# A new written order for the attention stage of a fused attention and mixer kernel

## The chip, the cores and the metric

The kernel runs on one core of a Trainium2 chip. What counts is the device time of one execution in microseconds (us), here the median of three runs. The core has five engines with their own queues, each in order: TensorE (matmuls), VectorE, ScalarE, GpSimd and SyncE (which only starts transfers).

## The reference

Three blocks follow each other, for 2 batches, 768 positions and 512 features.

```python
# 1. attention, 8 heads of 64: keys and queries count only within one hash bucket
mask = q_bucket[:, :, :, None] == k_bucket[:, :, None, :]      # 6 sign bits of x @ proj
scores = np.where(mask, scale * q @ k.T, -1e9)
attn = exp(scores - max) / (sum + 1e-9);  x = attn @ v
# 2. first mixer
xk, xr = mu * x + (1 - mu) * x_prev                            # x_prev: one position earlier
x = sigmoid(xr @ w_r) * (relu(xk @ w_k) ** 2 @ w_v)
# 3. second mixer: x @ w_in, norm, product over positions with w_spatial, gate, @ w_out
```

## The kernel before

Everything is fp32; a product of weights is made of three fp32r products of high and low parts (`mm3`). The weights come as float64 words and are unpacked on the chip by eight steps (`weight_jobs`): load, magnitude (ScalarE), clamp, shift, top (VectorE), first (ScalarE), power, low (VectorE), rest (two operations on GpSimd for the weights of attention's time, on VectorE later).

Attention goes over 8 pairs of heads, 12 units to a pair (2 halves of the queries x 2 heads x 3 blocks of 128 queries), 96 units in all. A group is six units. A unit is

- `scores` (S, line 394): 4 matmuls of 384 columns into one of two score banks `s`,
- `peak` (K, line 404, VectorE): scales the scores into `p` (three buffers) and takes the row's extreme; it frees the score bank,
- `expo` (X, line 416, ScalarE): the exponential in place, with its sum,
- `transp` (T, line 426): two groups of three 128x128 transposes, each group into one of three banks `t`; T2i and T2i+1 belong to unit i,
- `evac` (line 432): copies each bank `t` to `PT`, on ScalarE (E) or on VectorE (V).

When a group's units are evicted, `av3` (A, line 461) multiplies `PT` with the values: two calls per group, each 12 matmuls in the trace, into the one output bank `o`. `recip` (R) inverts the sums on VectorE and writes them to DRAM by four transfers, `spread` (D) reads them back to all partitions, and `finish` (F, line 473) multiplies the output bank into `XT` and frees it. For a coming pair there are loads of keys and queries to the `tk` tiles by GpSimd's queue (`load_pair`, four transfers), the raw load (`load_x`), the values (`load_v`), the hash bits (`bits_mm` Z, line 292, 8 matmuls into a bank `t`; `bits_signs` G on VectorE and GpSimd; `bits_place` B or P, transfers on SyncE's queue), and eight subtractions on GpSimd (`split_piece` Q, line 275).

The order of every queue is the order in which the program names the operations. Before, nine units are written out as a string `head`, and from the third period on a loop over periods of three units says

```python
scores(a); scores(a + 1); peak(a)
move(a - 2, 1); expo(a); move(a - 1, 0); move(a - 1, 1)
peak(a + 1); ...; expo(a + 1); av3(p - 3); ...
scores(a + 2); move(a, 0); move(a, 1); ...
```

where `move` is T and E in one; other jobs (weights, loads, mixing pieces of the first mixer) hang on slots of the periods (`plan`). After the loop the last products of attention stand among the first of the mixer (`r_products`). From then on jobs hang on ticks, one to each group of 12 matmuls of 512 columns.

Of the kernel before, what the change touches and what calls it, by code (L numbers as in the profile page):

```python
# [16 lines left out]
B, H, S, D = 2, 8, 768, 64  # L17
# [7 lines left out]
WARM_A, WARM_B = 6, 3  # L25
# [207 lines left out]
def attention(tc, nc, mid, wide, top, dram, ident, msc, omu, misc, cst_sb, pb, epsT, kq, vP, XT, TK0, wr, w_r, wk,  # L233
              w_k, w_v, ps_s, ps_t, obank, mix_jobs, r_products, r_sigmoid, tick, now, at_tick, plan_weight, wv, **_):
    PS = bass.MemoryType.PSUM
    with ExitStack() as ctx:
# [76 lines left out]
        def bits_signs(pp):  # L313
            bits_sign(pp)
            bits_scale(pp, nc.gpsimd)
# [103 lines left out]
            P[i] = c  # L419

        def transp(i, c):
            p = P[i] if c == 0 else P.pop(i)
            t = ps_t.tile([128, 512], F32, tag="t", name="t")
            for n in range(3):
                k0 = 128 * (3 * c + n)
                nc.tensor.transpose(t[:, 128 * n:128 * n + 128], p[:, k0:k0 + 128], ident)  # L426
            return t
# [48 lines left out]
                R.pop(g).rearrange("p n q -> p (n q)"),  # L476
            )

        plan = {}

        early = []

        def at_slot(p, k, job):
            plan.setdefault((p, k), []).append(job)

        def plan_early(p0, where):
            ld, jobs = weight_jobs(
                nc, mid, w_v[:128], lambda: (wv[0][:, 0, 0, :], wv[0][:, 1, 0, :]), nc.vector,
            )
            early.extend(jobs)  # L490
            plan_unit(p0, where, ld, jobs, (0, 1, 2, 3, 5, 6))
# [14 lines left out]

        np3 = nunits // 3
        units = [(wr, w_r, c, 0) for c in range(4)]
        units += [(wk, w_k, c, o) for o in (0, 512) for c in range(4)]
        late = ((-1, 1), (0, 0), (0, 0), (0, 0), (1, 0), (1, 0), (1, 0), (1, 0))  # L510
        soon = ((-1, 2), (-1, 0), (-1, 0), (0, 0), (1, 0), (1, 0), (1, 1), (1, 1))
        first = ((-1, 1), (0, 0), (0, 0), (1, 0), (1, 0), (1, 0), (3, 0), (1, 1))

        def plan_unit(p0, where, ld, jobs, keys=range(8)):
            at_slot(p0 - 3, 1, ld)
            for k in keys:
                at_slot(p0 + where[k][0], where[k][1], jobs[k])

        for n in range(12):
            dst, src, c, o = units[n]  # L520
            ld, jobs = weight_jobs(
                nc, mid, src[128 * c:128 * c + 128, o:o + 512],
                lambda dst=dst, c=c, o=o: (dst[:, 0, c, o:o + 512], dst[:, 1, c, o:o + 512]),
                nc.gpsimd,
            )
            plan_unit(4 + 2 * n, soon if n % 2 else late, ld, jobs)
        plan_early(np3 - 4, first)
        both, pieces = (nc.vector, nc.vector), []
        for c in range(4):
            for h, jobs in enumerate(mix_jobs(mid, 0, 0, c, 0, both + (nc.gpsimd,))):  # L530
                pieces.append(jobs)
        begun = (52, 53, 54, 57, 58, 59, 60, 61)
        ended = (55, 56, 57, 58, 59, 60, 61, 62)
        for k in range(2 * np3):
            for jobs, b, e in zip(pieces, begun, ended):
                if e == k:
                    at_slot(k // 2, k % 2, jobs[2])
            for jobs, b, e in zip(pieces, begun, ended):
                if b == k:
                    at_slot(k // 2, k % 2, jobs[0])  # L540
                    at_slot(k // 2, k % 2, jobs[1])
        gates1 = [jobs for c in range(4) for jobs in mix_jobs(mid, 1, 0, c, 4, both + (nc.vector,))]
        for pp in range(-1, npairs - 1):
            p0 = 4 * pp
            if pp >= 0:
                if pp:
                    at_slot(p0, 0, lambda n=pp + 1: load_pair(n))
                if pp:
                    at_slot(p0 + 1, 0, lambda n=pp + 1: bits_mm(n))
                    at_slot(p0 + 1, 0, lambda n=pp + 1: bits_signs(n))  # L550
                at_slot(p0 + 1, 1, lambda n=pp + 1: bits_place(n, (0, 1) if n > 1 else (0,)))
                at_slot(p0 + 3, 1, lambda n=pp + 1: load_v(n))
                for k in range(8):
                    at_slot(p0 + 1 + k // 4, k // 2 % 2, lambda n=pp + 1, k=k: split_piece(n, k))
            if 0 <= pp < npairs - 2:
                at_slot(p0 + 3, 0, lambda n=pp + 2: load_x(n))

        nc.scalar.dma_start(msc, misc)
        load_halves()
        clear(0, 0, nc.vector)  # L560
# [20 lines left out]
            for n in range(3):  # L581
                av(p // 2, 3 * (p % 2) + n)

        def move(i, c, copy=nc.scalar.copy):
            evac(i, c, transp(i, c), copy)

        ts = {}

        def group(k):
# [2 lines left out]
        def from_group(k, copy=nc.scalar.copy):  # L592
            evac(k // 2, k % 2, ts.pop(k), copy)

        def slot(n):
            for job in plan.pop((n // 10, n % 10), ()):
                job()

        step = {
            "S": scores, "K": peak, "X": expo, "T": group, "E": from_group,  # L600
            "V": lambda k: from_group(k, nc.vector.tensor_copy), "J": slot, "Z": bits_mm, "G": bits_signs,
            "L": lambda e: split_part(0, e, 0, nc.vector), "R": recip, "P": lambda e: bits_place(1, (e,)),
        }
        head = (
# [3 lines left out]
        )  # L608
        for w in head.split():
            step[w[0]](int(w[1:]))  # L610
            if w == "S1":
                warm(WARM_B)
        for p in range(3, np3):
            a = 3 * p
            scores(a)
            scores(a + 1)
            peak(a)
            if p > 3:
                move(a - 2, 1)
                expo(a)  # L620
                move(a - 1, 0)
                move(a - 1, 1)
            else:
                move(a - 1, 0)
                expo(a)
                move(a - 1, 1)
            peak(a + 1)
            for job in plan.pop((p, 2), ()):
                job()
            expo(a + 1)  # L630
            av3(p - 3)
            if p % 2 == 0:
                recip(p // 2 - 1)
            if p == 3:
                spread((p - 3) // 2, nc.gpsimd)
            for job in plan.pop((p, 0), ()):
                job()
            if p % 2 and p > 3:
                spread((p - 3) // 2, nc.sync)
            if p >= np3 - 2:  # L640
                tick()
            scores(a + 2)
            move(a, 0)
            move(a, 1)
            peak(a + 2)
            expo(a + 2)
            if p >= 4 and p % 2 == 0:
                finish((p - 4) // 2)
            move(a + 1, 0)
            for job in plan.pop((p, 1), ()):  # L650
                job()
            if p == np3 - 2:
                plan_wv()
            if p >= np3 - 2:
                tick()
        assert not any(p < np3 for p, _ in plan), plan

        def begin(*ns):
            for n in ns:
                gates1[n][0]()  # L660
                gates1[n][1]()

        def end(*ns):
            for n in ns:
                gates1[n][2]()

        o = r_products(0, 0)
        begin(0, 1)
        r_sigmoid(0, 0, o, top)
        move(nunits - 2, 1)  # L670
        move(nunits - 1, 0)
        move(nunits - 1, 1)
        recip(np3 // 2 - 1)
        begin(2)
        av3(np3 - 3)
        end(0, 1)
        begin(3)
        spread(np3 // 2 - 1, nc.sync)
        tick()
        o = r_products(0, 1)  # L680
        finish(np3 // 2 - 2)
        end(2, 3)
        begin(4, 5, 6)
        r_sigmoid(0, 1, o, top)
        tick()
        av3(np3 - 2)
        av3(np3 - 1)
        finish(np3 // 2 - 1)
        assert not plan, plan

    def rest_of_gates():
        end(4, 5, 6)
        begin(7)
        end(7)

    return rest_of_gates

# [311 lines left out]
```

## Time and profile before

| | us |
|---|---|
| median of 3 runs | 537.13 (537.05 to 537.41) |
| span of the profiled execution, first to last instruction | 534.7 |
| TensorE busy | 528.7 |
| VectorE busy | 366.8 |
| ScalarE busy | 333.9 |
| GpSimd busy | 142.0 |

Of the profiled execution the trace times the span alone; the median of the runs is 2.4 us longer. Attention takes the first 225 us of the span. A TensorE that is busy by the profile is not one at its peak, since matmuls are pipelined: the distance between the starts of two rows says what the first one costs.

### The profile page before, as it was taken

To read this page: it belongs to the slowest core of one execution; us is meant where nothing else is said; L and a number is where in the kernel's file an instruction comes from. 1 tells how busy PE (TensorE), PEld (TensorE's weight loads), DVE (VectorE), ACT (ScalarE), POOL (GpSimd) and SP (SyncE) were. 2 spreads that over 40 slices of the span, in tenths; PEclk is the share of its full clock that TensorE was granted. 3 is DMA by queue.
4 is the path that set the end of the run, shared out by engine and by line. 5 is a ranking of instruction groups with operands and counts; after the bars stand their busy time and mean duration, and the time that the engine had idled before them with its cause. 6 is when DMAs were issued, how large, how long until landed. Compare 5 with 4: busy or idle time off the path is not lost.

```text
span 534.7 us, 8278 instructions
## 1 busy us (share of the span) xinstructions
PE 528.7 (99%) x2886; PEld 425.4 (80%) x2886; DVE 366.8 (69%) x751; ACT 333.9 (62%) x702; POOL 142.0 (27%) x157
## 2 busy tenths in 40 slices
PE   8999999999999999999999999999999999999997
PEld 6777777777777677688888888888888889989896
DVE  8786969686868987699678587445784948734230
ACT  8988989898989799457666567364433543221221
POOL 7939494949494832000000000001100000000000
PEclk9999999999999999999999999999999999999999
DMA  8994929393939312110221021005343200010102
GB/s 224 151 236 97 254 74 242 88 254 80 242 92 247 87 40 56 55 39 2 78 71 55 34 78 48 32 1 167 109 163 106 76 0 1 0 40 21 59 21 99
DMA packets 20041, 51.06 MB, mean 95 GB/s; under 512 B 3776, under 2 KB 6656, under 8 KB 20000
## 3 DMA queue, kind: packets, MB, share of 16 engines
q1 hardware_dynamic: 13424, 31.17, 19.3%
q0 software_dynamic: 6144, 19.07, 17.5%
q8 instruction: 23, 0.38, 0.3%
q10 hardware_dynamic: 432, 0.28, 0.2%
q14 instruction: 18, 0.15, 0.1%
HBM read 46.29 MB, written 3.19 MB: 93 GB/s over the span
## 4 chain that ended last, share of the span: by engine, by line
PE 95%; DVE 2%; ACT 1%; issue 1%; DVEq 0%
PE o L183 14%; PE s L394 13%; PE v L764 12%; PE o L461 12%; PE t L426 11%; PE k L183 9%; PE s L183 7%; PE r L183 6%; PE w L183 6%; PE u L183 5%; PE z L292 1%; ACT p L416 1%; DVE p L404 1%; DVE tk L379 1%; DVE d L152 0%
## 5 line engine op out<-in xcount | busy, mean ns | idle before, releaser
L404 DVE TENSOR_SCALAR_CACHE_REDUCE p<-s 128x768 f32<-128x768 f32 x96 | 90.9, 955 | 37.0 <-PE s L394 34.4
L432 ACT COPY PT<-t 128x384 f32<-128x384 f32 x189 | 83.6, 479 | 20.2 <-PE t L426 20.0
L416 ACT ACTIVATE p<-p,m 128x768 f32<-128x768 f32 x96 | 90.7, 945 | 3.2 <-DVE p L404 2.3
L394 PE MATMUL s<-tk 128*128 128x384 f32 x384 | 85.0, 354 | 0.9 <-DVE p L404 0.4
L394 PEld LDWEIGHTS s<-tk 128*128 128x128 f32 x384 | 63.9, 188 | 19.7 <-issue 6.0
L426 PE MATMUL t<-ident,p 128*128 128x128 f32 x576 | 74.9, 273 | 0.5 <-ACT p L416 0.5
L426 PEld LDWEIGHTS t<-ident,p 128*128 128x128 f32 x576 | 66.6, 141 | 5.4 <-ACT p L416 1.7
L764 PE MATMUL v<-k,wv 128*128 128x512 f32 x288 | 68.9, 389 | 0.0
L461 PE MATMUL o<-PT,v 128*64 128x384 f32 x384 | 68.8, 494 | 0.0
L764 PEld LDWEIGHTS v<-k,wv 128*128 128x128 f32 x288 | 54.0, 188 | 11.2
L275 POOL TENSOR_TENSOR tk<-x,tk 64x384 fp32r<-64x384 f32 x56 | 58.9, 1079 | 1.0
L821 POOL DMA_DIRECT2D wsp<-in_w_spT_dram x6 | 3.3, 564 | 169.9 <-DVE w_a L45 155.3
L461 PEld LDWEIGHTS o<-PT,v 128*64 128x64 f32 x384 | 24.8, 136 | 28.6 <-issue 27.9
L750 DVE TENSOR_TENSOR k<-kt,k 128x512 fp32r<-128x512 f32 x24 | 16.6, 691 | 30.7 <-ACT k L749 30.6
L183 PE MATMUL k<-tk,wk 128*128 128x512 f32 x144 | 35.6, 389 | 0.0
L183 PE MATMUL o<-wk,tk 128*128 128x512 f32 (+1 forms) x162 | 34.9, 374 | 0.0
L130 ACT CAST tk<-g 128x384 fp32r<-128x384 f32 x16 | 8.2, 513 | 42.0 <-DVE g L896 42.0
L183 PEld LDWEIGHTS o<-wk,tk 128*128 128x128 f32 x162 | 28.9, 188 | 5.3
L183 PEld LDWEIGHTS k<-tk,wk 128*128 128x128 f32 x144 | 27.0, 188 | 5.6
L156 DVE SCALAR_TENSOR_TENSOR f<-XT,msc,d 128x256 f32<-128x256 f32 x48 | 24.5, 510 | 6.0 <-ACT d L150 4.6
L66 DVE SCALAR_TENSOR_TENSOR w_a<-w_raw,w_p 128x512 f32<-128x512 uint32 x32 | 26.6, 831 | 0.9
L183 PE MATMUL w<-wk,tk 128*128 128x512 f32 x114 | 26.5, 389 | 0.0
(131 smaller groups left out, 847.8 us busy)
## 6 DMA issues: line engine op xcount, KB each, us to landing
tk<-in_kq_dram POOLq DMA_DIRECT2D x30, 384.0 KB, 9.5
x<-in_kq_dram POOLq DMA_DIRECT2D x6, 768.0 KB, 5.6
w_raw<-in_w_k_dram SPq DMA_DIRECT2D x8, 512.0 KB
w_raw<-in_w_v_dram SPq DMA_DIRECT2D x8, 512.0 KB
w_raw<-in_w_in_dram SPq DMA_DIRECT2D x8, 512.0 KB
v<-in_vP_dram SPq DMA_DIRECT2D x8, 384.0 KB
rb<-ds SPq DMA_DIRECT2D x30, 96.0 KB
out_dram<-ot SPq DMA_DIRECT2D x11, 256.0 KB
```

What stands on the lines that cost most here:

```text
L66: nc.vector.scalar_tensor_tensor(st["a"].bitcast(F32), st["raw"][:, :, 0], 2.0 ** -52, st["p"].bitcast(F32), op0=ALU.mult, op1=ALU.mult,)
L156: nc.vector.scalar_tensor_tensor(st["f"], x, mu, st["d"], op0=ALU.mult, op1=ALU.add)
L183: nc.tensor.matmul(o, a, x, start=(i == 0), stop=(i == len(seq) - 1))
L275: nc.gpsimd.tensor_sub(tk[l, 1 + 2 * t, o], raw[pp][l, t, o], tk[l, 2 * t, o])
L394: nc.tensor.matmul(s[:, c, :HS], w, t[:, n, c * HS:(c + 1) * HS], start=(n == 0), stop=(n == 1),)
L404: nc.vector.tensor_scalar(c, s[:, :, :HS], -0.125, BIG / 16, op0=ALU.mult, op1=ALU.min, accum_out=m)
L416: nc.scalar.activation(c, c, AF.Exp, bias=m, scale=-1.0, accum_out=den[g][:, u:u + 1])
L426: nc.tensor.transpose(t[:, 128 * n:128 * n + 128], p[:, k0:k0 + 128], ident)
L432: copy(PT[g][:, e, 3 * c:3 * c + 3, 128 * j:128 * j + 128], t[:, :HS].rearrange("p (n q) -> p n q", n=3),)
L461: nc.tensor.matmul(obank[64 * e:64 * e + 64, :HS], vt[g // 2][:, kt, e, :], PT[g][:, e, kt, :], start=(kt == 0), stop=(kt == 5),)
L750: held.append(lambda kk=k2[i]: nc.vector.tensor_sub(kk[:, 1], t, kk[:, 0]))
L764: nc.tensor.matmul(o, w, x, start=(c == 0 and k == 0), stop=(c == 7 and k == 2))
```

## The change

From the middle of the head on, the string, the loop over periods and its plan of slots are replaced by one written list of 1004 operations for all 96 units. A letter names the operation (as above; W n.k is step k of weight n, M and N the two halves of a mixing piece of the first mixer, b and e the same for its second block, p and s the first products of the mixer and their sigmoid, t a tick, Y the plan of the value weights, L, x, v the loads). What is computed stays as it was. The calls of A stand next to each other on TensorE's queue more often: 20 runs instead of 31. 37 evictions are V instead of 3. From unit 18 to 65 the list repeats itself every twelve units; before, it repeated itself every three, with slots that differ within twelve. Two of the weights of the second product of the first mixer (`w_v`) are unpacked later: their ticks go from 1 to 4 and from 8 to 9.

```diff
-            if p > 3:
-                move(a - 2, 1)
-                expo(a)
-                move(a - 1, 0)
-                move(a - 1, 1)
...
                     plan_weight(
-                        (0, 1, 8, 11, 14, 16, 18, 21)[n], (wv[h][:, 0, c, :], wv[h][:, 1, c, :]),
+                        (0, 4, 9, 11, 14, 16, 18, 21)[n], (wv[h][:, 0, c, :], wv[h][:, 1, c, :]),
...
+        def mix(n):
+            pieces[n][0]()
+            pieces[n][1]()
...
+            "V": lambda k: from_group(k, nc.vector.tensor_copy), "Z": bits_mm, "G": bits_signs,
+            "L": load_pair, "B": bits_place, "x": load_x, "v": load_v, "Q": split_piece, "W": unit,
+            "A": av3, "F": finish, "D": lambda g: spread(g, nc.sync if g else nc.gpsimd),
+            "M": mix, "N": lambda n: pieces[n][2](), "t": lambda n=0: tick(), "Y": lambda n=0: plan_wv(),
...
+S0 S1 w3 K0 S2 K1 X0 T0 X1 l1 T1 T2 K2 E0 S3 E1 E2 T3 K3 X2 S4 E3 K4 Z1 G1 T4 V4 X3 X4 S5 W0.0 T5 T7 W0.1 K5
+T6 E5 S6 E7 W0.2 K6 S7 W0.3 T8 E6 T9 X5 E8 K7 W1.0 R0 X6 S8 v1 T10 E9 T11 K8 E10 S9 T13 W1.1 Q1.2 X7 T12 Q1.1
+A0 K9 E12 X8 V11 Q1.3 V13 T14 T17 T15 Q1.0 S10 E14 S11 T16 P0 V17 X9 Q1.7 E16 T19 E15 P1 K10 V19 X10 A1 K11
...
+X28 Q3.6 E53 X29 A6 A7 W3.6 T54 T55 E52 W3.7 W4.0 S30 D3 E54 E55 T56 B3 x4 T57 K30 E56 S31 T59 T58 E57 X30 K31
+S32 V58 E59 T61 X31 T60 E61 v3 K32 S33 T62 V60 K33 X32 W5.0 T63 S34 E63 T65 V62 K34 X33 E65 S35 X34 T64 T67
+T66 S36 K35 S37 K36 E64 T69 E67 F3 T68 S38 W2.8 R4 E66 K37 D4 X35 T70 E69 T71 A8 E70 R5 W4.1 A9 E68 W4.2 E71
+W3.5 Z4 W4.3 X36 T72 L4 T73 W3.8 W4.4 K38 X37 G4 S39 E72 Q4.2 W4.6 S40 T74 X38 T75 W4.7 Q4.1 K39 E73 Q4.3 T77
+W5.1 Q4.4 E74 F4 W4.5 Q4.5 Q4.7 X39 S41 W5.2 K40 E75 Q4.0 T76 W5.3 K41 W5.4 X40 Q4.6 E77 X41 A10 A11 W5.6 T78
+T79 E76 W5.7 W6.0 S42 D5 E78 E79 T80 B4 x5 T81 K42 E80 S43 T83 T82 E81 X42 K43 S44 V82 E83 T85 X43 T84 E85 v4
+K44 S45 T86 V84 K45 X44 W7.0 T87 S46 E87 T89 V86 K46 X45 E89 S47 X46 T88 T91 T90 S48 K47 S49 K48 E88 T93 E91
...
+E143 M1 K74 Z7 A21 E142 M2 T144 T145 W10.3 G7 S75 W10.4 X73 V144 T146 X74 T147 E145 W11.0 E146 T148 W9.5 K75
...
+E183 T182 T181 N7 F13 A28 V182 D14 K93 b0 A29 E181 K94 X93 T184 b1 e0 W11.6 X94 T188 S95 T187 E188 V184 T185
+E187 T186 W12.2 b2 W11.5 E186 K95 p0 F14 e1 E185 X95 T190 E190 R15 Y t T189 T191 b3 e2 e3 E191 W11.7 D15 t b4
+E189 W12.3 A30 A31 t W11.8 p1 b5 W12.4 W12.6 W12.7 t F15 s0 t s1 t b6
```

## Rows read from the trace of the kernel before

**Rows 1.** The page: busy shares; a GpSimd group; a transfer's size and landing.
```profile
PE 528.7 (99%) x2886; PEld 425.4 (80%) x2886; DVE 366.8 (69%) x751; ACT 333.9 (62%) x702; POOL 142.0 (27%) x157
...
L275 POOL TENSOR_TENSOR tk<-x,tk 64x384 fp32r<-64x384 f32 x56 | 58.9, 1079 | 1.0
...
tk<-in_kq_dram POOLq DMA_DIRECT2D x30, 384.0 KB, 9.5
```
**Rows 2.** Windows: stretch and length; busy PE, PEld, DVE, ACT, POOL; clock; DMA share, GB/s.
```profile
10.00:23.80 13.80, 13.56 (x96) 11.17 (x94) 11.86 (x25) 13.19 (x32) 13.32 (x18) 1.00 1.10 232
30.00:80.00 50.00, 50.00 (x337) 36.38 (x335) 37.49 (x82) 43.71 (x99) 32.45 (x33) 1.00 0.74 171
```
**Rows 3.** Timeline of TensorE, 98 to 105: start, duration, line, operation, tiles, instructions.
```profile
98.28 0.98 PE L394 MATMUL s<-tk 128*128 128x384 f32 x4
99.10 1.14 PE L426 MATMUL t<-ident,p 128*128 128x128 f32 x9
100.00 1.66 PE L394 MATMUL s<-tk 128*128 128x384 f32 x8
101.50 1.14 PE L426 MATMUL t<-ident,p 128*128 128x128 f32 x9
102.57 2.16 PE L461 MATMUL o<-PT,v 128*64 128x384 f32 x12
104.66 0.97 PE L394 MATMUL s<-tk 128*128 128x384 f32 x4
```
**Rows 4.** The chain that ended last, in order of time: start, time, line, instructions.
```profile
23.88 2.09 PE o L461 x12
...
220.99 4.02 PE o L461 x24
...
271.51 2.72 PE v L764 x12
```
**Rows 5.** Timeline of TensorE, 177 to 192; in brackets a wait and its releaser.
```profile
177.04 0.98 PE L394 MATMUL s<-tk 128*128 128x384 f32 x4
...
180.11 0.97 PE L394 MATMUL s<-tk 128*128 128x384 f32 x4 [0.41 <-DVE p L404]
...
186.08 0.55 PE L426 MATMUL t<-ident,p 128*128 128x128 f32 x3 [0.30 <-ACT p L416]
...
191.21 0.97 PE L394 MATMUL s<-tk 128*128 128x384 f32 x4
```
**Rows 6.** Timeline of all engines, 10 to 30 (PEld: weight loads).
```profile
12.36 0.49 PE L426 MATMUL t<-ident,p 128*128 128x128 f32 x3
...
12.60 0.94 PE L394 MATMUL s<-tk 128*128 128x384 f32 x4
...
13.47 0.85 PE L292 MATMUL z<-x,msc 128*32 128x384 f32 x8
...
14.25 0.55 PE L426 MATMUL t<-ident,p 128*128 128x128 f32 x3
...
14.55 0.94 PE L394 MATMUL s<-tk 128*128 128x384 f32 x4
...
19.71 1.02 DVE L432 COPY PT<-t 128x384 f32<-128x384 f32 x2
...
20.32 0.31 PEld L426 LDWEIGHTS t<-ident,p 128*128 128x128 f32 x3 [0.16 <-DVE PT L432]
```
**Rows 7.** Timeline of ScalarE, 184 to 185.
```profile
184.27 0.84 ACT L432 COPY PT<-t 128x384 f32<-128x384 f32 x2
```
**Rows 8.** Timeline of VectorE, 182 to 184.
```profile
182.34 0.94 DVE L404 TENSOR_SCALAR_CACHE_REDUCE p<-s 128x768 f32<-128x768 f32 x1
...
183.22 0.95 DVE L404 TENSOR_SCALAR_CACHE_REDUCE p<-s 128x768 f32<-128x768 f32 x1
```
**Rows 9.** Line 66 (a weight's long step), 30 to 170: shortest, median, longest, ns.
```profile
L66 DVE SCALAR_TENSOR_TENSOR w_a<-w_raw,w_p x11: 691/693/1583, 37.4 to 168.7; 128x512 f32<-128x512 uint32 x11
```
**Rows 10.** Timeline of VectorE, 254 to 255 (the third value weight's last step).
```profile
254.56 0.69 DVE L78 TENSOR_TENSOR wv<-w_b,w_a 128x512 fp32r<-128x512 f32 x1
```

More of the change, by code (lines that the diff above doesn't have):

```diff
@@ L421, in transp @@
         def transp(i, c):
[L422 removed]
+            p = P[i]
             t = ps_t.tile([128, 512], F32, tag="t", name="t")
@@ L477, in finish @@
             )
[L479 to L486, printed above, removed]
+        units = [(wr, w_r, c, 0) for c in range(4)]
+        units += [(wk, w_k, c, o) for o in (0, 512) for c in range(4)]
+        steps = []
+        for dst, src, c, o in units:
             ld, jobs = weight_jobs(
-                nc, mid, w_v[:128], lambda: (wv[0][:, 0, 0, :], wv[0][:, 1, 0, :]), nc.vector,
-            )
-            early.extend(jobs)
-            plan_unit(p0, where, ld, jobs, (0, 1, 2, 3, 5, 6))
+                nc, mid, src[128 * c:128 * c + 128, o:o + 512],
+                lambda dst=dst, c=c, o=o: (dst[:, 0, c, o:o + 512], dst[:, 1, c, o:o + 512]),
+                nc.gpsimd,
+            )
+            steps.append([ld] + jobs)
+        ld, early = weight_jobs(
+            nc, mid, w_v[:128], lambda: (wv[0][:, 0, 0, :], wv[0][:, 1, 0, :]), nc.vector,
+        )
+        steps.append([ld] + early)
         def plan_wv():
@@ L507, in attention @@
         np3 = nunits // 3
[L508 to L527, printed above, removed]
         both, pieces = (nc.vector, nc.vector), []
         for c in range(4):
-            for h, jobs in enumerate(mix_jobs(mid, 0, 0, c, 0, both + (nc.gpsimd,))):
-                pieces.append(jobs)
@@ L532, in attention @@
[L532 to L541, printed above, removed]
-        gates1 = [jobs for c in range(4) for jobs in mix_jobs(mid, 1, 0, c, 4, both + (nc.vector,))]
@@ L543, in attention @@
[L543 to L556, printed above, removed]
+            pieces += mix_jobs(mid, 0, 0, c, 0, both + (nc.gpsimd,))
@@ L604, in attention @@
-        head = (
[3 rows of a table removed]
[L608 to L617, printed above, removed]
-            if p > 3:
-                move(a - 2, 1)
-                expo(a)
-                move(a - 1, 0)
-                move(a - 1, 1)
[L623 to L676, printed above, removed]
@@ new lines, in attention, with gate @@
+            "l": lambda e: split_part(0, e, 0, nc.vector), "R": recip, "P": lambda e: bits_place(1, (e,)),
+            "L": load_pair, "B": bits_place, "x": load_x, "v": load_v, "Q": split_piece, "W": unit,
+            "A": av3, "F": finish, "D": lambda g: spread(g, nc.sync if g else nc.gpsimd),
+            "M": mix, "N": lambda n: pieces[n][2](), "t": lambda n=0: tick(), "Y": lambda n=0: plan_wv(),
+        }
+        step["w"] = warm
+        held = {}
+        def gate(n):
+            held[n] = r_products(0, n)
@@ new lines, in mix1 @@
+        def mix1(n):
+            gates1[n][0]()
+            gates1[n][1]()
+        step.update({
+            "p": gate, "s": lambda n: r_sigmoid(0, n, held.pop(n), top),
+            "b": mix1, "e": lambda n: gates1[n][2](),
+        })
+        order = """
+S0 S1 w3 K0 S2 K1 X0 T0 X1 l1 T1 T2 K2 E0 S3 E1 E2 T3 K3 X2 S4 E3 K4 Z1 G1 T4 V4 X3 X4 S5 W0.0 T5 T7 W0.1 K5
+T6 E5 S6 E7 W0.2 K6 S7 W0.3 T8 E6 T9 X5 E8 K7 W1.0 R0 X6 S8 v1 T10 E9 T11 K8 E10 S9 T13 W1.1 Q1.2 X7 T12 Q1.1
+A0 K9 E12 X8 V11 Q1.3 V13 T14 T17 T15 Q1.0 S10 E14 S11 T16 P0 V17 X9 Q1.7 E16 T19 E15 P1 K10 V19 X10 A1 K11
@@ new lines, in attention @@
+T120 L6 T121 W7.8 W8.4 K62 X61 G6 S63 E120 Q6.2 W8.6 S64 T122 X62 T123 W8.7 Q6.1 K63 E121 Q6.3 T125 W9.1 Q6.4
+E122 F8 W8.5 Q6.5 Q6.7 X63 S65 W9.2 K64 E123 Q6.0 T124 W9.3 K65 W9.4 X64 Q6.6 E125 X65 A18 A19 W9.6 T126 T127
+E124 W9.7 W10.0 S66 B6 E126 E127 K66 T129 E129 T128 E128 S67 W8.8 T131 K67 X66 T130 S68 x7 V131 E130 T133 X67
+S69 D9 E133 T132 E132 K68 T135 T134 K69 X68 V135 F9 X69 S70 S71 T137 K70 R10 T136 V136 A20 K71 E134 W10.1
+W10.2 E137 T138 X70 T139 X71 L7 E138 T141 S72 E139 S73 M0 D10 E141 T140 T143 R11 E140 K72 X72 T142 K73 S74
@@ L696, in attention @@
+E189 W12.3 A30 A31 t W11.8 p1 b5 W12.4 W12.6 W12.7 t F15 s0 t s1 t b6
+"""
+        for w in order.split():
+            step[w[0]](*(int(n) for n in w[1:].split(".") if n))
+    def rest_of_gates():
+        for n in (4, 5, 6):
+            gates1[n][2]()
+        gates1[7][0]()
+        gates1[7][1]()
+        gates1[7][2]()
     return rest_of_gates
```

45 lines of the change are left out of this document (22 added, 23 removed), and 3 rows, old and new, of the table head.

## The prediction

> **What bounds the kernel now.** Read the page's busy shares first: TensorE is busy 99% of the span, the others 69% and less [rows 1]. That alone says little, since matmuls overlap, so the windows come next: in attention TensorE is busy 50.00 of 50 us at full clock, ScalarE 43.7, VectorE 37.5, GpSimd 32.5 [rows 2]. The timeline of TensorE then shows that this is work and not waiting. One period of three units is s x4, t x9, s x8, t x9, o x12, and it comes back after 6.38 us, without one wait that is named [rows 3]. What the change can give in attention is therefore what TensorE's own sequence costs beyond its matmuls, and the few places where it does wait.
>
> Two costs of the sequence can be read off. Nine transposes last 0.90 us to the next instruction when scores follow, and 1.07 when a value product follows [rows 3]: turning to a value product costs 0.17. Twelve value matmuls last 2.09 us (102.57 to 104.66), two runs back to back 4.02 [rows 3, 4], so the second run costs 1.93, and 0.16 is the price of leaving value products. One run fewer saves 0.17 + 0.16 = 0.33 us. Changing between scores and transposes is near free: a t to s change takes less than a transpose's own step.
>
> TensorE waits in one stretch. From 177.04 to 191.21 two periods take 14.17 us where 2 x 6.38 = 12.76 would do: 1.4 us, first for a score bank that VectorE has not read (0.41), then for an exponential (0.30) [rows 5]. VectorE has the first mixer's token mixing there besides its peaks.
>
> After attention TensorE goes from one group of 12 matmuls to the next every 2.72 us [rows 4]. What attention saves is then saved at the end, if nothing after it was waiting for another engine.
>
> **The change part by part.**
>
> *Runs of value products.* Before, 32 calls make 31 runs (only the last two stand together). In the new list 8 stand alone and 12 pairs have nothing of TensorE's between them: 20 runs. Every call keeps its 12 matmuls. 11 runs fewer x 0.33 = **3.6 us saved**. After a value run come transposes in 14 cases, where before scores came. The trace has no such pair. Its nearest row is three transposes after hash bits: 0.30 us, against 0.24 for three after scores [rows 6], 0.06 more. What a first score pays after a value run is of that size, so I take no difference; the bounds are 0.1 less (loads hidden) to 0.2 more each, that is 1.4 us better to 2.8 worse.
>
> *Evictions.* 34 of 192 move from ScalarE to VectorE (3 were there already). ScalarE loses 34 x 0.42 = 14 us [rows 7], VectorE gains 34 x 0.51 = 17 us [rows 6]. Neither is on the path if they keep up. In the repeating twelve units (S30 to S41) TensorE has 4 x 6.38 + 0.78 for the hash bits (13.47 to 14.25 [rows 6]) - 2 x 0.33 = 25.6 us of work. The same twelve took 26.3 us before, in which VectorE was busy 26.3 x 37.5 / 50 = 19.7 and ScalarE 23.0 us [rows 2]; 3 evictions moved make that 21.2 and 21.7. Both have a seventh left or more, so it is a matter of order inside the period.
>
> *Order inside the period.* Units 30 to 37 now run with no value product among them, about 1.4 us each, and the pairs A8 A9 and A10 A11 stand in the next eleven microseconds. I went through the list by hand: scores 0.70, a transpose group 0.33, a peak 0.88 [rows 8] from 0.25 after its scores, and each short step of VectorE at 0.69, the usual duration of a weight's long one [rows 9]. From S36 at 0: T71 ends at 3.4, A8 A9 at 7.6, Z4 8.4, T73 9.05, S40 10.45, T77 11.45. VectorE: K37 to 3.8, R5 4.5, three steps of a weight to 6.6, K38 to 7.5, G4 after Z4 to 9.3, two more steps to 10.7, K39 to 11.55. S41 takes the bank that K39 reads, and wants it at 11.45: 0.1 us late. That is the tightest place, and each of the four periods has it. F4 follows at 12.25; A10 wants its output bank at 12.6. In the run of units without value products each eviction on VectorE (V82, V84, V86) is done 0.7 to 1.1 us before the transpose that takes its buffer, the third after its own. If that cover were gone the transpose would wait, and the scores behind it in TensorE's queue.
>
> *GpSimd and the queues.* GpSimd's 32.5 of 50 us [rows 2] are 17.1 per period, and now nearly all of it stands in the half with the value pairs, where TensorE has 17.4. L4 can go at S35's end (-1) and lands some 9.5 us after each issue [rows 1], by 11; G4 holds GpSimd's queue until Z4 is read (9.3); eight splits of 1.08 [rows 1] then end near 20, and S48 reads them at 25.6. SyncE's eight placings (B4) stand behind D5, which waits for F4 (12.25), and have 13 us until then. Both cost nothing; without that cover the scores of a new pair would wait. At the start the load W1.0 moves ahead of P0 and P1 and shares the DMA engines with the second pair's loads. At 232 GB/s [rows 2] its 0.5 MB delays them 2.3 us. By the same count S12 comes near 29.7 and the four splits that it reads end near 26.5; P0 and P1 now stand behind R0's four writes instead of around them, and end together with them as before. So no change there; the few waits of the first periods I take as equal in both orders.
>
> *The stretch with waits.* The mixing pieces are spread from S72 to S93, beside or just after value runs, instead of from period 26 on. Walked the same way from S66 the list shows no wait longer than 0.1 us. The closest are T147, whose buffer V144 frees 0.2 us before, and A28, for which F13 must be done, 0.4 us before. So I count the **1.4 us as recovered**.
>
> One row is against trusting that whole: a weight step that takes 0.69 us has taken 1.58 [rows 9], and the weight steps now stand in the half where GpSimd is busy. The Trainium skill, SBUF — State Buffer, Who interferes with whom, says that a VectorE instruction with two SBUF inputs fully blocks against a GpSimd one that reads SBUF, whichever comes first. By that rule every weight step beside a split would be held, and the time would be the second rival's below. The row's median, 0.69, bears the rule out for a few of them only. I take **0.8 us of new waits**: 0.4 at S41 in four periods, and one stretched step of 0.4 in the tail; bounds 0 and 3.
>
> *Two value weights later.* The second's steps move 3 ticks (8.2 us) on, the third's 1 (2.7). On the old time line the third begins its last step at 254.56 [rows 10] and would at 257.3; its product begins at 271.51 [rows 4]. 13 us of value products and keys hide it; without that cover it would cost one group of 2.72.
>
> **Sum.** 3.6 + 1.4 - 0.8 = 4.2 us off the profiled span of 534.7, which stands 2.4 under the median of 537.13. The rest does not move: **532.9 us**.
>
> **The rivals.**
>
> *The evictions on VectorE are late (slower).* TensorE waits at the transposes that need their buffers. At the two that stand back to back at 19.71, TensorE's weight loads waited 0.16 us for the first [rows 6], 0.08 for each. At that price 34 cost 2.7 us: 535.6, still faster. It decides from (3.6 + 1.4) / 34 = 0.15 us each; at 0.3 the time is 537.1 - 5.0 + 10.2 = 542.3. For it: VectorE's queue is in order and each eviction stands behind a peak. Against: ring of three buffers and the spare times above.
>
> *Weight steps and splits block each other (little gained).* If each of the ten steps in every repeating period is stretched as the worst one by 0.9 us, VectorE has 21.2 + 9 = 30 us against 25.6, and the four periods would lose 18. With one stretched step ahead of K39 in each, S41 waits 1.0 instead of 0.1, and with as much twice in the tail 5.6 us go: 532.9 + 5.6 - 0.8 = 537.7. The usual row says less; I put this at 535 to 537.7.
>
> *The turnaround is only moved.* A first transpose after a value run costs 0.3 more than a first score; 14 x 0.3 = 4.2, 537.1. For it: unseen pair. Against: the hash-bit row.
>
> *The clock falls.* Where transposes and scores run without value products TensorE would be granted the lower of its levels (1.2 instead of 2.4 GHz): eleven microseconds in each of four periods twice as long, +44 us, 577. Against: from 10 to 23.8 us no value product runs (the first starts at 23.88) and the clock granted is 1.00, the 2.4 GHz level [rows 2, 4]. The Trainium skill, TensorE: Matmul & The Clock Gate, Part 4, says that transposes do not count as a busy TensorE; the trace does not bear that out here.
>
> **How the numbers follow.** The forecast has 0.76 (531.2 to 535), weights and splits 0.12, the moved turnaround 0.05, late evictions 0.05, the clock 0.02. Faster needs more than 0.2% (1.1 us, below 536.06), about what can be told from no change: 0.76 of the forecast, 0.09 of the second rival and 0.03 of the small ends of the others = 0.88. Within 0.2% 0.07, slower 0.05. The range: below, no new waits and half of the hidden loads, 532.9 - 0.8 - 0.7 = 531.4, say 531.2; above, 3 us of new waits and the small turnaround bound, 532.9 + 2.2 + 0.7 = 535.8.
>
> **What would show it.** In the timeline after: runs o x24 of about 4.0 us, and the repeating twelve units at 25.5 to 25.7 us from z to z instead of 26.25; t x6 after o x24 with no more than 0.1 on its first step; no wait for p on VectorE in the tail; S41's places at under 0.2 us. Wrong would be: waits of transposes for evictions on VectorE, weight steps with means near 1 us, splits that end after the scores that want them, or a granted clock under 1.00.

## The result and the profile after

The kernel after takes **542.12 us** (median of 4 runs, 540.97 to 542.57); the kernel before took 537.24 beside it. The ratio is 1.0091 [1.0079, 1.0103]: slower, where 532.9 was forecast. The profiled execution has a span of 540.2, 5.5 us more than before.

The busy shares on the page of the kernel after answer to [rows 1]:

```profile
PE 528.9 (98%) x2886; PEld 426.1 (79%) x2886; DVE 382.5 (71%) x785; ACT 321.2 (59%) x668; POOL 144.0 (27%) x157
```

The windows answer to [rows 2]: the repeating twelve units, fifty microseconds of attention, and ten of them in steps of two (columns as there).

```profile
91.35:116.83 25.48, 25.48 (x178) 19.30 (x176) 22.21 (x46) 21.91 (x49) 19.22 (x19) 1.00 0.70 171
...
50.00:100.00 50.00, 46.93 (x305) 33.01 (x303) 39.23 (x83) 37.91 (x86) 33.46 (x33) 0.93 0.70 174
...
66.00:68.00 2.00, 0.04 (x2) 0.04 (x2) 0.65 (x2) 0.00 (x0) 2.00 (x3) 0.77 0.25 83
68.00:70.00 2.00, 2.00 (x8) 0.79 (x10) 2.00 (x4) 0.00 (x0) 1.87 (x3) 0.50 0.80 283
...
72.00:74.00 2.00, 2.00 (x10) 0.77 (x8) 1.97 (x2) 0.69 (x3) 1.90 (x3) 0.53 0.62 123
74.00:76.00 2.00, 2.00 (x15) 1.24 (x12) 1.49 (x1) 0.51 (x2) 0.94 (x1) 1.00 0.86 313
```

Two things are to be seen. Where nothing waits, the new list does what it should: the twelve units from one z to the next take 25.48 us with TensorE busy throughout (25.6 forecast, 26.25 before). But from 50 to 100 TensorE is busy 46.93 of 50, and its granted clock is 0.93. In this stretch the loss has one place: TensorE stands still around 66, and then runs at 0.50, its level of 1.2 GHz instead of 2.4, until about 74.

The timeline of TensorE in the kernel after shows this place, and its twin two blocks of twelve units later (60 to 76 and 118 to 130), against [rows 3]:

```profile
64.40 0.49 PE L426 MATMUL t<-ident,p 128*128 128x128 f32 x3
67.96 7.01 PE L461 MATMUL o<-PT,v 128*64 128x384 f32 x24 [3.07 <-DVE XT L473]
74.90 0.88 PE L426 MATMUL t<-ident,p 128*128 128x128 f32 x6
...
121.43 0.49 PE L426 MATMUL t<-ident,p 128*128 128x128 f32 x3
123.86 5.79 PE L461 MATMUL o<-PT,v 128*64 128x384 f32 x24 [1.94 <-DVE XT L473]
129.58 0.66 PE L426 MATMUL t<-ident,p 128*128 128x128 f32 x4
```

These are A6 A7 and A14 A15. Three transposes ahead of a value product take 0.42 to the next start where nothing waits (loads_small below, 63.91 to 64.33); here 3.56 and 2.43, so 3.14 + 2.01 us of standing still. The products behind take 6.94 and 5.72 instead of 4.02: another 2.92 + 1.70. Together 9.8 us, and forecast and result are 9.2 apart.

What A6 waits for is F2 (line 473), which frees the output bank. The timeline of VectorE in the kernel after says when R2's last step is done and what F2 waits for:

```profile
55.05 0.21 DVE L444 STREAM_TRANSPOSE rt<-rc 128x32 f32<-128x32 f32 x1
...
67.35 0.56 DVE L473 TENSOR_TENSOR XT<-o,rb 128x384 f32<-128x384 f32 x1 [3.81 <-DMA rb<-ds]
```

It is the reciprocal's way back from DRAM. The chain of the kernel after follows it, and one more row of it answers to [rows 4]:

```profile
56.30 7.64 DMA ds<-rt
64.52 2.74 DMA rb<-ds
67.96 7.01 PE o L461 x24
...
96.44 4.02 PE o L461 x24
113.25 6.54 DMA ds<-rt
```

R2's four small writes (0.8 KB each) leave SyncE at 55.30 and have landed 7.64 us after the last; only then can D2 read them back, in 2.74. Just ahead of them GpSimd's queue had issued L3, four transfers of 384 KB (the last of them beside the first write):

```profile
53.58 0.62 POOL L263 DMA_DIRECT2D tk<-in_kq_dram  x1
...
55.35 0.62 POOL L264 DMA_DIRECT2D tk<-in_kq_dram  x1
```

In the page of the DMA engines for that stretch (53 to 66, kernel after) the loads' queue took 82% of the 16 engines' time, and the loads land 8.6 us after their issue:

```profile
q0 software_dynamic: 700, 2.24, 82.3%
...
tk<-in_kq_dram POOLq DMA_DIRECT2D x4, 384.0 KB, 8.6
```

The kernel before had the same slow way back, but for another group. Its timeline of SyncE, on which the prediction does not rest, shows R2 and D2, then R3 and D3:

```profile
50.46 1.41 SPq L447 DMA_DIRECT2D ds<-rt  x4
52.89 1.15 SPq L454 DMA_DIRECT2D rb<-ds  x2
...
58.16 1.29 SPq L447 DMA_DIRECT2D ds<-rt  x4
66.51 1.27 SPq L454 DMA_DIRECT2D rb<-ds  x2
```

For R3 it is 8.35 us from write to read, behind a load issued at 57.08. But F3 stood at 73.92, 15.8 us after the writes, and the next value product at 76.32. R2 was read back ahead of that load. It was done on VectorE at 44.53, 18.3 us before the product that wants the bank (timelines of VectorE and TensorE in the kernel before):

```profile
44.53 0.21 DVE L444 STREAM_TRANSPOSE rt<-rc 128x32 f32<-128x32 f32 x1
```

```profile
62.79 2.16 PE L461 MATMUL o<-PT,v 128*64 128x384 f32 x12
```

The new list has R2 done at 55.05, 9.8 us before A6 wants the bank (64.82), and behind the load instead of ahead of it. So the theory: **the list writes the reciprocals of the even groups later than the loop did, close ahead of a pair of value products and behind a load, and leaves them less time than the way through DRAM then takes**; and TensorE, having stood still, is then granted its lower clock.

### The profile page after: what moved, and what is told of

Same layout as the page of the kernel before. It is cut to its first block, busy times and chain, and to the rows that moved or that the text cites. A ratio compares the mean times of both kernels' runs of the same rounds, so it can differ in the third digit from the quotient of the medians.

```text
span 540.2 us, 8240 instructions
## 1 busy us (share of the span) xinstructions
PE 528.9 (98%) x2886; PEld 426.1 (79%) x2886; DVE 382.5 (71%) x785; ACT 321.2 (59%) x668; POOL 144.0 (27%) x157
## 4 chain that ended last, share of the span: by engine, by line
PE 88%; DMA 6%; POOL 2%; SPq 1%; issue 1%; DVE 1%; ACT 0%; DVEq 0%; POOLq 0%
PE o L183 14%; PE v L696 12%; PE o L461 11%; PE t L426 9%; PE s L394 9%; PE k L183 9%; PE s L183 7%; PE r L183 6%; PE w L183 6%; PE u L183 5%; DMA ds<-rt 3%; DMA tk<-in_kq_dram 1%; DMA rb<-ds 1%; DMA tk<-zc 1%; SPq L326 1%; PE z L292 1%
## 5 line engine op out<-in xcount | busy, mean ns | idle before, releaser
L432 ACT COPY PT<-t 128x384 f32<-128x384 f32 x155 | 69.8, 476 | 33.3 <-PE t L426 33.1
L394 PE MATMUL s<-tk 128*128 128x384 f32 x384 | 86.7, 355 | 0.8 <-DMA tk<-zc 0.5
L426 PE MATMUL t<-ident,p 128*128 128x128 f32 x576 | 79.6, 275 | 0.6 <-DVE zb L299 0.3
L461 PE MATMUL o<-PT,v 128*64 128x384 f32 x384 | 71.0, 518 | 5.0 <-DVE XT L473 5.0
L461 PEld LDWEIGHTS o<-PT,v 128*64 128x64 f32 x384 | 27.2, 144 | 39.4 <-issue 33.6
```

Source lines behind the costliest of these rows:

```text
L394: nc.tensor.matmul(s[:, c, :HS], w, t[:, n, c * HS:(c + 1) * HS], start=(n == 0), stop=(n == 1),)
L432: copy(PT[g][:, e, 3 * c:3 * c + 3, 128 * j:128 * j + 128], t[:, :HS].rearrange("p (n q) -> p n q", n=3),)
L461: nc.tensor.matmul(obank[64 * e:64 * e + 64, :HS], vt[g // 2][:, kt, e, :], PT[g][:, e, kt, :], start=(kt == 0), stop=(kt == 5),)
```

## The experiments

Of the written list the edits show only the piece that changes; where the same is done for several pairs, one of them stands for all.

| run | us (range) | ratio to before |
|---|---|---|
| loads_small | 531.81 (531.66–531.85) | 0.9900 [0.9884, 0.9917] |
| before_small | 537.28 (536.90–537.70) | 1.0000 [0.9991, 1.0009] |
| before_r_late | 548.99 (545.64–551.61) | 1.0221 [1.0170, 1.0273] |
| keep_busy | 539.94 (539.14–540.50) | 1.0051 [1.0036, 1.0066] |
| r_early | 544.50 (543.28–545.60) | 1.0137 [1.0119, 1.0155] |
| split | 544.43 (544.02–545.50) | 1.0138 [1.0123, 1.0153] |
| split_rb2 | 540.07 (537.91–543.50) | 1.0058 [1.0034, 1.0082] |
| early_back | 541.38 (540.71–547.42) | 1.0104 [1.0049, 1.0158] |
| runs_alone | 555.05 (554.95–555.35) | 1.0335 [1.0319, 1.0350] |
| small_scalar_evict | 537.31 (536.92–538.07) | 1.0007 [0.9998, 1.0016] |
| small_wv | 532.05 (531.82–532.76) | 0.9908 [0.9891, 0.9924] |
| late_loads | 538.60 (536.87–540.31) | 1.0026 [1.0012, 1.0040] |
| late_loads_start | 538.16 (536.70–540.05) | 1.0019 [1.0005, 1.0032] |
| late_two | 544.26 (542.19–545.05) | 1.0123 [1.0104, 1.0142] |
| late_three_v4 | 538.05 (535.87–540.43) | 1.0012 [1.0000, 1.0025] |
| late_four | 533.83 (532.57–534.84) | 0.9935 [0.9921, 0.9948] |
| late_five | 535.07 (534.57–535.76) | 0.9963 [0.9951, 0.9976] |

### Are the loads the cause?

**loads_small**, **before_small**: the kernels after and before, but of the keys and queries of pairs 3 to 7 only 8 of 768 columns are loaded (the rest of the work is done on what stands in the tiles).

```diff
-                src = kq[b, p][:, 64 * (1 - e):64 * (1 - e) + 64].rearrange("t d s -> d t s")
-                t = TK[pp % 2][e]
+                cut = 8 if pp > 2 else S
+                src = kq[b, p][:, 64 * (1 - e):64 * (1 - e) + 64].rearrange("t d s -> d t s")[:, :, :cut]
+                t = TK[pp % 2][e][:, :, :cut]
```

> The changed kernel; of the keys and queries of the fourth pair and later only 8 of 768 columns are loaded into the tk tiles, so that these transfers are nearly empty (its output is another one). Theory A with the loads as the reason for the lateness: the four writes of the reciprocals land within 3 us instead of 7.5, no wait before A6 and A14, 532 to 533 us. A without the loads (the way through DRAM is too long by itself): the waits stay, at least 2 us each with the clock falling, 538 to 542. Rival B: 541 to 542.

> The kernel before with nearly empty loads from the fourth pair on (output another one). If the loads cost the kernel before nothing, since its reciprocals have two periods until the finish: 537 us within 0.5. If they held it too: 533 to 536, and the new order's gain with empty loads would be smaller than the 5.4 us that it looks like.

The new list gains all that it lost, and the old one is unmoved. In loads_small the timeline of SyncE has the read 3.5 us after the write, and TensorE's has A6 without a wait:

```profile
54.82 1.30 SPq L448 DMA_DIRECT2D ds<-rt  x4
58.31 1.16 SPq L455 DMA_DIRECT2D rb<-ds  x2
```

Timeline of TensorE, loads_small:

```profile
63.91 0.49 PE L427 MATMUL t<-ident,p 128*128 128x128 f32 x3
64.33 4.09 PE L462 MATMUL o<-PT,v 128*64 128x384 f32 x24
```

So the loads are the cause, and in the new list only; without them the sum of the prediction stands: 531.8 against 532.9.

**before_r_late**: the kernel before with each group's reciprocal one period later, next to its way back. All else is the old order.

```diff
-            if p % 2 == 0:
-                recip(p // 2 - 1)
+            if p % 2 and p > 3:
+                recip((p - 3) // 2)
```

> The kernel before with one thing undone, the distance: each reciprocal one period (6.4 us) later, next to its way back, the finish where it was. If the distance from reciprocal to finish was what covered the loads in the kernel before: TensorE waits for finishes, at least 1 us in each group of a pair whose loads are under way, and where it stands some 3 us its clock falls: 542 to 560 us. If not: 537.

The old order gets the same stall as soon as the distance is short, here behind a wait of 6.72 us of VectorE for `rb` (timeline of TensorE, before_r_late):

```profile
94.02 3.47 PE L461 MATMUL o<-PT,v 128*64 128x384 f32 x10 [4.96 <-DVE XT L473]
```

Here it is the read that meets the load: D4 leaves at 84.19, the load from 83.27 on, and F4 starts at 93.41. Pairing is not needed for the stall; how late R and D stand, and behind which load, decides.

### Is the slow product the clock's?

**keep_busy**: the kernel after, with 14 and 9 products of the identity, two records each in the trace, into one of the three banks `t` ahead of A6 and A14, so that TensorE has something to do while it waits (added work, not part of the computation).

```diff
-X28 Q3.6 E53 X29 A6 A7 W3.6
+X28 Q3.6 E53 X29 u14 A6 A7 W3.6
```

> The changed kernel with 14 and 9 extra products of the identity (about 2.8 and 1.8 us, result unused) in the two long waits before A6 and A14. If the clock falls because TensorE stands still there: the waits stay but the clock stays at 1.00, the slow value runs (6.94 and 5.72 us) come back to 4.02, 542.1 - 4.6 = 537.5 us. If the clock falls for another reason, or the slow runs are themselves waits: 542 or more.

In TensorE's timeline of keep_busy the product behind takes 4.02 again (68.75 to 72.77):

```profile
65.43 3.39 PE L568 MATMUL t<-ident 128*128 128x128 f32 x28 [0.88 <-ACT PT L432]
68.75 4.09 PE L461 MATMUL o<-PT,v 128*64 128x384 f32 x24
72.77 0.87 PE L426 MATMUL t<-ident,p 128*128 128x128 f32 x6
```

The mean clock rises from 0.991 to 0.998 and 2.2 us come back, less than the 4.6 that the two slow products cost. At A6 the added products end with the wait; at A14 F6 was done at 121.16 in this run and the added products only at 123.53, 2.4 us later. The clock is a consequence of the standing still.

### Does the way back come through if it, or the loads, start earlier?

**r_early** moves the four late reciprocals R2, R4, R6, R8 ahead of the eight placings B; **split** issues each load in two halves, both some units earlier; **split_rb2** adds to split that R and D of these groups stand behind the load of the values, with a second tile for `rb`; **early_back** has R, four placings, D, four placings, and the second tile.

```diff
-W2.0 S18 D1 E30 E31 T32 B2
+W2.0 S18 D1 E30 E31 T32 R2 B2
...
-S26 W0.8 R2 E42 K25 D2 X23
+S26 W0.8 E42 K25 D2 X23
```

Split (h is half a load) and, in the last lines, split_rb2; early_back (c is half of the placings):

```diff
-x3 T33 K18 E32 S19 T35 T34 E33 X18 K19 S20 V34
+x3 T33 K18 E32 S19 T35 T34 E33 X18 K19 S20 h3.0 V34
...
-T41 V38 K22 X21 E41 S23 X22
+T41 V38 K22 X21 E41 S23 h3.1 X22
...
-E37 v2 K20 S21
+E37 v2 R2 D2 K20 S21
...
-S18 D1 E30 E31 T32 B2
+S18 D1 E30 E31 T32 R2 c2.0 D2 c2.1
```

> The changed kernel with the reciprocals R2, R4, R6, R8 about 10 us earlier, each before the placings of its period. Theory A (the finish of a group waits for its reciprocals, whose way through DRAM starts too late and lands behind the next pair's loads; the wait then costs again through the clock): both long waits and both stretches at the lower clock go, 542.1 - 9.7 = 532.4 us. Rival B (two pairs of value runs stand too close for the one output bank, whatever the transfers do): TensorE still waits some 3 and 2 us before A6 and A14, 541 to 542. Rival C (evictions on VectorE come late): no change, 542.

> The changed kernel; of each later pair's four loads the two for the first head are issued as soon as the scores of unit 20, 32, 44, 56 or 68 have read their tile, the other two after unit 23, 35, 47, 59 or 71, both ahead of the weight remainder that stood before them in GpSimd's queue. If what counts is that the reciprocals' small transfers land behind these loads: loads some 3 us earlier leave at most 2 us of wait before A6 and A14, the clock falls less or not, 534 to 538 us. If it counts that reciprocals start late: 541 to 543 as changed.

> The same, and the reciprocals R2, R4, R6, R8 with their way back D2, D4, D6, D8 stand after the load of the values, some 4 us earlier; the odd groups of these keep their reciprocals in another tile, so that D no longer has to wait for the finish before. If the way through DRAM behind the loads is the cause: no wait before A6 and A14, 532 to 533 us. If early transfers are held by the loads whatever their place: waits as in split or more.

> The changed kernel with the loads where they were, but R2, R4, R6, R8 ahead of the placings of the first head and D2, D4, D6, D8 between these and the second's; the odd groups up to the seventh keep their reciprocals in another tile, so that D waits for no finish. The whole way through DRAM is then over or ahead of the loads: by the same theory no wait before A6 and A14, 532 to 535 us (the placings are 2 to 4 us later and may hold a pair's first scores). If being early did not help: 540 and more, as with the reciprocals alone early.

None of the four reached the kernel before. In r_early the writes come early, but D2 has to wait until F1 (54.63) has read the one tile `rb`, meets the load (from 54.08 on), and F2 waits as long as ever, 3.87 us, until 67.95. The placings are later too, and scores wait 1.82 us for them at 87.24.

In split the loads leave GpSimd at 50.30 to 52.06, 3.3 us sooner, which only puts more of them ahead of the writes: 9.2 us from write to read (timeline of SyncE):

```profile
54.58 1.29 SPq L447 DMA_DIRECT2D ds<-rt  x4
63.80 1.16 SPq L454 DMA_DIRECT2D rb<-ds  x2
```

In split_rb2 and early_back F is no longer what ends the wait. Another transfer is: a weight's raw words on SyncE's queue, which ScalarE needs ahead of its next eviction. Timeline of ScalarE, early_back:

```profile
68.23 0.66 ACT L42 ACTIVATE w_a<-w_raw 128x512 f32<-128x512 f32 x1 [5.39 <-DMA w_raw<-in_w_r_dram]
```

TensorE waits 4.84 us there for the eviction behind it. The words were issued at 55.04, behind L3, and landed 13.1 us later. In split_rb2 the wait at this place is 2.56, in one of the fastest of its ten runs (537.95); there the words stand in SyncE's queue behind D2, which waits for its writes until 59.38, and leave only at 60.63. What is issued behind the loads is late, be it the way back or a weight, and so is what stands in a queue behind it.

### The parts of the change by themselves

**runs_alone** pairs the value products in the order before (every second period issues two), and changes nothing else; **small_scalar_evict** is loads_small with 34 of the 37 evictions on ScalarE again; **small_wv** is loads_small with the value weights' old ticks.

```diff
-            av3(p - 3)
+            if p % 2 == 0:
+                av3(p - 4)
+                av3(p - 3)
```

Of the others:

```diff
-S32 V58 E59 T61 X31 T60 E61 v3 K32 S33 T62 V60
+S32 E58 E59 T61 X31 T60 E61 v3 K32 S33 T62 E60
```

```diff
-                        (0, 4, 9, 11, 14, 16, 18, 21)[n], ...
+                        (0, 1, 8, 11, 14, 16, 18, 21)[n], ...
```

> The kernel before with one part of the change alone: the two value runs of a group stand together in every second period, 16 runs instead of 31, everything else as it was. If a run saved is worth 0.33 us and nothing else waits: 15 x 0.33 = 5 us less, 532.2. If the uneven periods (8.2 and 4.1 us of TensorE's work) outrun ScalarE in the short ones (about 5.5 us of work): some 1 us of wait in each of 14, 546 or more.

> The changed kernel with nearly empty loads from the fourth pair on (531.8 us in the run before, output another one), and 34 of the 37 evictions on ScalarE again. Theory: without the stalls ScalarE has work for 23 of 25.6 us in twelve units and the first eight of them hold no value product, so transposes wait for its evictions: 2 to 6 us more, 534 to 538. Rival: the evictions' engine does not matter, 531.8.

> The changed kernel with nearly empty loads from the fourth pair on, and the two value weights at their old ticks (1 and 8). Theory: the weights are hidden either way, 531.8 us within 0.3. Rival: they were moved since VectorE is full at the end of attention: 533 or more.

Pairing alone costs 18 us: with 15 runs fewer at 0.33 it should have saved 5, so some 23 us of waits came in. Windows of runs_alone, 50 to 100: TensorE is busy 45.50, at full clock, and a wait at a transpose comes back in every period, 1.36 us for the hash bits' sign or 0.76 for an exponential in turn:

```profile
50.00:100.00 50.00, 45.50 (x305) 33.78 (x303) 34.64 (x78) 41.02 (x95) 28.12 (x30) 1.00 0.70 162
```

Timeline of TensorE, runs_alone:

```profile
99.06 0.52 PE L426 MATMUL t<-ident,p 128*128 128x128 f32 x3 [1.36 <-DVE zb L299]
```

The evictions on VectorE are worth 5.5 us (537.31 - 531.81) in the new list. Without them ScalarE is no fuller than before on the whole, 43.21 of 50 us against [rows 2], but waits before transposes come back (nine of them take 1.51 us at 104.63, where 1.14 is usual). The value weights are worth nothing either way: 532.05 and 531.81, intervals that overlap.

### Loads later, behind the reciprocals

**late_loads** puts L3 to L7 behind the hash scale G of their pair, which on GpSimd's queue comes some 9 us later and behind the reciprocal's way back, and starts the splits with the half that lands first. **late_loads_start** adds P0 ahead of R0 and V4 ahead of the sign G1.

```diff
-X24 T48 L3 T49 W1.8 W2.4 K26 X25 G3 S27
+X24 T48 T49 W1.8 W2.4 K26 X25 G3 L3 S27
```

> The changed kernel; the loads L3 to L7 stand behind the hash scale (G) in GpSimd's queue, so that they are issued some 8 us later, after the reciprocals of the even groups are back, and the splits of the first head come before those of the second. If small transfers issued behind these loads land only when the loads have: no wait before A6 and A14, no stretch at the lower clock, 532 to 533 us. If the splits now come late: waits of scores at the start of a pair, 534 to 540.

> As late_loads, and at the start the first head's placings P0 ahead of R0 and the eviction V4 ahead of the sign of the hash bits. The wait of 0.9 us before the first scores of the second pair goes, and some of the 0.6 us of waits near 16 us: 1 us less than late_loads, 531 to 532 us. If these waits are covered by others: the same as late_loads.

Both stalls are gone, and 3.5 us come back, but a new one stands at 153 to 160 in the profiled run (537.55). Timelines of GpSimd, ScalarE and TensorE in late_loads, in this order:

```profile
151.90 3.89 POOL L275 TENSOR_TENSOR tk<-x,tk 64x384 fp32r<-64x384 f32 x4 [1.12 <-DMA tk<-in_kq_dram]
...
157.10 1.26 POOL L78 TENSOR_TENSOR wk<-w_b,w_a 128x512 fp32r<-128x512 f32 x1
```

```profile
158.40 0.66 ACT L42 ACTIVATE w_a<-w_raw 128x512 f32<-128x512 f32 x1 [4.61 <-POOL wk L78]
```

```profile
156.75 0.55 PE L426 MATMUL t<-ident,p 128*128 128x128 f32 x3
159.48 0.55 PE L426 MATMUL t<-ident,p 128*128 128x128 f32 x3 [2.19 <-ACT PT L432]
```

The splits, late with their loads, hold the remainder of a weight (W8.8) on GpSimd, the next weight's first step waits for it on ScalarE, and the eviction behind that step comes late. The start's own waits shrink by a few tenths.

**late_two** has only L3 and L5 late, in the same way, the two that stalled; **late_three_v4** L3 to L5, and V4 ahead of G1.

> The changed kernel; only the loads of the fourth and sixth pair (L3, L5), those that the two long waits met, stand behind the hash scale, with the first head's splits first; the other loads stand as changed. If those two meetings of loads and reciprocals are the whole loss, with full loads and a correct output: 532 to 533 us, like the kernel with nearly empty loads. If moving the loads only moves the trouble (a later queue on GpSimd, as in late_loads): 535 to 540.

> The same with L4 late too, and V4 ahead of the sign of the hash bits at the start: 0.5 us less than late_two if L4 meets nothing, 531.5 to 533; some us more if GpSimd's queue is then late for the eighth weight, as in late_loads.

late_two is the clearest miss: slower than the kernel after. The stalls are now at A10 and A18, where the kernel after had none. Timelines of late_two, GpSimd, SyncE, TensorE:

```profile
82.16 0.62 POOL L263 DMA_DIRECT2D tk<-in_kq_dram  x1
```

```profile
81.38 1.30 SPq L447 DMA_DIRECT2D ds<-rt  x4
86.76 1.14 SPq L454 DMA_DIRECT2D rb<-ds  x2
```

```profile
94.96 5.46 PE L461 MATMUL o<-PT,v 128*64 128x384 f32 x22 [3.94 <-DVE XT L473]
```

L4 leaves within a microsecond of R4's writes there. In the kernel after it left at 79.49 and the writes only at 86.77: the stall at A6 had let GpSimd run ahead of TensorE, and so spared the next block. Cure the first and the second has it. late_three_v4 fits: its only large wait is at A18, whose L6 is still early (2.77 us, then 1.7 of slow products).

**late_four**: L3 to L6 late, L7 where it was, V4 and P0 as in late_loads_start, and W8.8 ahead of the splits of L6's pair. **late_five** has L7 late too.

```diff
-T120 L6 T121 W7.8 W8.4 K62 X61 G6 S63 E120 Q6.2 W8.6
+T120 T121 W7.8 W8.4 K62 X61 G6 L6 S63 E120 W8.6
...
-E122 F8 W8.5 Q6.5 Q6.7
+E122 F8 W8.5 W8.8 Q6.2 Q6.1 Q6.3 Q6.0 Q6.5 Q6.7
```

> Theory (the way back F waits only because the pair's loads stand ahead of it on the DMA engines; a moved load shifts the wait to the next block that still loads early): with L3 to L6 behind their hash scales, L7 where it was, the remainder of weight 8 ahead of the sixth pair's splits and P0 ahead of R0, neither A6, A14, A10 nor A18 waits; less than 5 us of extra time is left in attention and the time is 533 to 534.5, faster than before. Rival (the new list has no room for the loads anywhere, whichever place is free): a stall of 3 to 6 us appears at another place and the time is 537 to 540.

> The same with L7 late too. Theory: 533 to 535, the stall at 153 to 158 that the version with all loads late had is gone, since the remainder of weight 8 no longer stands behind the splits. Rival: GpSimd is late as a whole after its loads, the stall stays at 3 us and the time at 537 to 538.5.

late_four is faster than both kernels, by 0.65% [0.52, 0.79] than before. Timelines of SyncE and of GpSimd in late_four show why: the read stands 2.8 us behind the write, and the load leaves after both.

```profile
54.74 1.30 SPq L447 DMA_DIRECT2D ds<-rt  x4
57.52 1.16 SPq L454 DMA_DIRECT2D rb<-ds  x2
```

```profile
62.26 0.65 POOL L263 DMA_DIRECT2D tk<-in_kq_dram  x1
```

The splits then end later, and the scores that read them still do not wait. At 110 late_four is level with loads_small (hash bits at 110.36 and 110.34). What is left, 3.0 us in the profiled runs, comes after: 0.6 by 116, the rest around waits of 0.86, 0.33 and 0.40 us between 154 and 172. With L7 late too 1.2 us are lost again, though the ranges of the two just overlap; scores then wait 1.58 us at 181.64 for a split of the last pair.

## Why the prediction was wrong

*The step that failed* is the part on GpSimd and the queues: "L4 can go at S35's end (-1) and lands ... by 11", "SyncE's eight placings (B4) stand behind D5, which waits for F4 (12.25) ... Both cost nothing". Two terms are missing from it. The walk gave F4 only its place on VectorE's queue ("F4 follows at 12.25"), and with it F2, F6 and F8, which stand alike; it did not ask when the reciprocal, on its way through DRAM by R and D, is back. And the loads of the repeating units were held only against the splits that wait for them, never against the small transfers on the same DMA engines. From the end of R2 to the product that wants the bank it was 18.3 us and is 9.8, and the way takes 12.3 behind a load (55.05 to 67.35 after). The trace of before had the way: 8.35 us from write to read for R3. Loss: 5.2 us of standing still.

*The clock* was a rival with the wrong condition. It was priced for transposes and scores without value products, and these are granted 1.00 here, before [rows 2] and after (91.35 to 116.83). The prediction took the first of these to speak against transposes as a cause; neither tests transposes by themselves, since a unit has 0.70 us of scores to 0.66 of transposes. What lowered it was TensorE standing still: after the stops of 3.1 and 2.0 us the products ran at the 1.2 GHz level for part of their time, and with added work in the stops they did not. Loss: 4.6 us.

*Fewer runs, 3.6 us; the tail's 1.4 recovered; the turnaround not moved.* All three agree with the rows, though no run has one of them alone. The pairs take 4.02, t x6 after a value run costs 0.63 (184.26 - 183.63), 0.06 more than after scores (185.05 to 185.62), and in the tail, against [rows 5], TensorE goes without a named wait (timeline of the kernel after):

```profile
179.61 4.09 PE L461 MATMUL o<-PT,v 128*64 128x384 f32 x24
183.63 0.87 PE L426 MATMUL t<-ident,p 128*128 128x128 f32 x6
184.26 0.94 PE L394 MATMUL s<-tk 128*128 128x384 f32 x4
```

With the loads out of the way the whole change is worth 5.4 us (537.2 - 531.81); 4.2 were forecast. The 0.8 for new waits at S41 and in the tail were not needed; 0.4 of the gain is not accounted for.

*Evictions on VectorE are late:* no. They are worth 5.5 us. The pairs are no gain by themselves: in the old order they cost 18 (runs_alone, whose waits are not for evictions). In the new order with the evictions on ScalarE and the loads small the time is 537.31, level with before, so, as far as the two can be set side by side (16 runs there, 20 here), the order takes back what pairing costs and the evictions let the gain come through. The prediction costed the evictions at nothing and gave the whole gain to the pairs and the tail.

*Weight steps and splits:* the sign that was named came, without harm. Line 66 in the kernel after, against [rows 9]:

```profile
L66 DVE SCALAR_TENSOR_TENSOR w_a<-w_raw,w_p x10: 679/956/1666, 38.0 to 155.2; 128x512 f32<-128x512 uint32 x10
```

Its median rose from 693 to 956 ns. VectorE had 22.21 of 25.48 us, 1 more than reckoned, and TensorE has no named wait for it. The Trainium skill's rule (SBUF — State Buffer, Who interferes with whom) fits these rows better than those of before, yet the price at TensorE was nought.

*Value weights later:* hidden, as said.

## What to carry over

When an order is rewritten, list for every buffer the whole way that must come back before the next use, transfers included, and set the new distance, of the same group, against the longest time that this way takes in the old trace, beside its worst neighbour. A stall shifts the queues behind it: curing one uncovers the next (late_two), and a fix at all places can open another (late_loads), so every place of the pattern is looked at again. Price a stop of TensorE with what the clock takes after it, here nearly as much again.

## What the hardware showed

Small transfers pay for large ones issued ahead of them from another queue: four writes of 0.8 KB were read back 3.5 us later with nearly empty loads and 8.7 us (55.30 to 63.96) behind 1.5 MB of loads. The read alone took 2.74 us after the loads and 6.94 behind them (late_two, from 87.32). The Trainium skill, DMA: Bandwidth & Descriptors, Queues, rings and completion order, says that a completion signal lands only after every earlier write of the same DMA engine, across its queues; the direction agrees, and no run here separates that from a plain sharing of the engines.

After the stops of 3.1 and 2.0 us TensorE was granted half its clock for several microseconds, which turned a wait of 3.1 into a loss of 6.1. Not every such stop does it. In late_loads TensorE stood still for 2.2 us, from 157.30 to 159.48, and the granted clock stayed at 1.00 (windows of late_loads):

```profile
157.00:166.00 9.00, 6.35 (x46) 4.37 (x46) 6.35 (x18) 7.27 (x17) 1.98 (x3) 1.00 0.51 154
```

At the same place in late_loads_start a wait of 1.94 us was followed by a granted 0.50 from 161 to 164. So the length of a stop of about 2 us does not tell by itself what comes after it, and one kernel's runs differ: late_loads took from 536.87 us at a mean granted clock of 1.000 to 540.31 at 0.993.
